# One stream of score blocks over all groups, PV per 256 queries in two accumulators, V per two groups, and an order planned with modelled engine clocks

## The chip, the cores and the metric

The kernel runs on one core of one Trainium2 chip, in one launch. The metric is the device time of the whole program in microseconds (us). The core's engines run side by side and wait for each other by semaphores: TensorE (PE, with its weight loads listed as PEld), VectorE (DVE), ScalarE (ACT), GpSimd (POOL) and SyncE (SP), which issues nearly all DMAs.

## The reference

Two problems, A and B, of the same form and independent of each other; the two results stand side by side in the output. S = 2048 tokens, D = 1024, 32 heads of 32, bf16, a causal window of 256 tokens:

```
qkv = x @ wqkv                       # [2048, 3072]; q, k, v of 32 heads of 32
scores = q @ k^T * 32**-0.5          # where 0 <= i - j < 256, else -1e9
o = softmax(scores) @ v              # per head
out = o (heads side by side) @ wo    # [2048, 1024]
```

## The kernel before

A group is four heads, 128 columns of q, k or v; a problem has T = 8 groups, the program 16 (G). The sequence is cut into 16 blocks of 128 tokens (NB) and four quarters of 512 (NQ). x is loaded transposed, a quarter a time (xT). Each projection is a chain of 8 steps over the inner dimension, and each step is four matmuls side by side, one for each 32 columns of its weights (`by_columns`, L127): q and k of a group for a quarter (`qk_steps`, L132), v for 128 tokens and four groups at once (`v_steps`, L152), and the output product (`out_steps`, L169). A chain of 512 columns sums in one PSUM bank, a tile `pp`, of which there are two; then a cast takes it to SBUF, by DVE for q and k (L145), by ACT for v and the output (L165, L183). After the cast of q or k DVE also takes the bitwise OR of it into `top` (L146), from which the kernel later decides if all q and k were small enough for a softmax without a maximum (`certify`, L571; a slow path follows if not).

The scores of a group are 45 pairs of a key block and a query block (`entries`). `session` (L276) takes four pairs, SLOTS: matmuls for the four heads into the four banks of the one tile `st`, one exponential on ACT for all of them (L298) into a tile `pt`, and masks on POOL (L303, L307). A group has 12 such score blocks, the last with a single pair: 192 in all, 16 of them with one pair. `pv` (L311) multiplies with v (and with ones, for the sums) for a quarter's 512 queries into the one tile `acc`, two banks; then DVE takes four reciprocals and two products (L342, L346) into oT, in pieces (`side`) which are handed out between projection steps.

The order is planned while the program is built. Every projection chain has an earliest and a latest score block. In front of each score block `forced` finishes what is due; behind it come the PV that is due (two blocks after its last exponential, PV_LAG), the loads, and then `emit` hands out steps up to a budget of `level` (L264): the larger of what must still be done and what may be done, spread evenly over the rest. Costs are constants per step (NS_MM, NS_QK, NS_PV). All loads and the output DMAs go through SP's queue in program order.

Of the kernel before, what the change touches and what calls it, by code (L numbers as in the profile page):

```python
# [18 lines left out]
P = 128  # L19
# [7 lines left out]
QB = 4  # L27
SLOTS = 4
NS_MM = 216.0
NS_QK = 430.0  # L30
NS_PV = 56.0
PV_LAG = 2
FREE = 10 ** 6

# [14 lines left out]
class _Chain:  # L49
    def __init__(self, early, late, steps):  # L50
        self.early, self.late, self.steps = early, late, steps


def _fast_path(ctx, tc, cfg, problems, outs, consts, certify):
# [5 lines left out]
    SB = 512 // P  # L60
    ones = consts["ones"]

    entries = [(j, q) for j in range(NB) for q in range(j, min(j + 3, NB))]
    place = {e: divmod(n, SLOTS) for n, e in enumerate(entries)}
    NS = -(-len(entries) // SLOTS)
    ready = [max(place[(j, q)][0] for (j, q) in entries if q // QB == k) for k in range(NQ)]

    def first_use(k, of):
        return min(place[e][0] for e in entries if e[of] // QB == k)
# [3 lines left out]
    wvp = ctx.enter_context(tc.tile_pool(name="wv", bufs=1))  # L73
    wopool = ctx.enter_context(tc.tile_pool(name="wo", bufs=1))
    opool = ctx.enter_context(tc.tile_pool(name="oT", bufs=NQ + 2))
# [6 lines left out]
    ps_acc = ctx.enter_context(tc.tile_pool(name="ps_acc", bufs=1, space=PSUM))  # L82
# [26 lines left out]
    def load_wv(m, queue, parts=1):  # L109
        pi, mm = divmod(m, T // SB)  # L110
        wv[m] = wvp.tile([P, CT, 512], BF16, name="wv")
        n = CT // parts
        for a in range(parts):
            queue.dma_start(out=wv[m][:, a * n:(a + 1) * n, :],
                            in_=wsrc(pi)[:, a * n:(a + 1) * n, 2, mm * 512:(mm + 1) * 512])

    def load_wo(pi):
        wo_sb[pi] = wopool.tile([P, CT, D], BF16, name="wo_sb")
        nc.sync.dma_start(out=wo_sb[pi][:],
                          in_=problems[pi][2].rearrange("(ct p) n -> p ct n", p=P))  # L120
# [6 lines left out]
    def by_columns(out, lo, hi, lhsT, rhs, start, stop):  # L127
        for c in range(0, P, 32):
            nc.tensor.matmul(out[c:c + 32, lo:hi], lhsT=lhsT[:, c:c + 32], rhs=rhs, start=start,  # L129
                             stop=stop, tile_position=(0, c))  # L130

    def qk_steps(g, which, k, lo=0, hi=512, st_=None, last=True):  # L132
        pi = g // T
        st_ = {} if st_ is None else st_
        steps = []
        for ct in range(CT):
            def f(ct=ct):
                if "pp" not in st_:
                    st_["pp"] = ps_proj.tile([P, 512], F32, name="pp")
                w_ = wqk[g][:, ct, which, :]  # L140
                by_columns(st_["pp"], lo, hi, lhsT=w_, rhs=xT[(pi, k)][:, ct, lo:hi],
                                 start=(ct == 0), stop=(ct == CT - 1))
                if ct == CT - 1 and last:
                    dst = qk_tiles(g)[which][:, k * 512:(k + 1) * 512]
                    nc.vector.tensor_copy(out=dst, in_=st_["pp"][:])  # L145
                    nc.vector.tensor_tensor(out=top[:], in0=top[:],  # L146
                                            in1=dst.bitcast(I32), op=ALU.bitwise_or)
            steps.append((NS_MM * (hi - lo) / 512.0, f))
        return steps

    def v_steps(m, b):
        pi = m // (T // SB)  # L152
# [3 lines left out]
        for ct in range(CT):  # L156
            def f(ct=ct):
                if ct == 0:
                    st_["pp"] = ps_proj.tile([P, 512], F32, name="pp")
                    if (m, k) not in vts:  # L160
                        vts[(m, k)] = vp.tile([P, QB, 512], BF16, name="vt")
                by_columns(st_["pp"], 0, 512, lhsT=xT[(pi, k)][:, ct, a * P:(a + 1) * P],
                                 rhs=wv[m][:, ct, :], start=(ct == 0), stop=(ct == CT - 1))
                if ct == CT - 1:
                    nc.scalar.copy(out=vts[(m, k)][:, a, :], in_=st_["pp"][:])  # L165
# [3 lines left out]
    def out_steps(pi, b, ch, osb):  # L169
        k, a = divmod(b, QB)  # L170
        st_ = {}
        steps = []
        for ct in range(CT):
            def f(ct=ct):
                if ct == 0:
                    st_["pp"] = ps_proj.tile([P, 512], F32, name="pp")
                    if ch == 0:
                        osb[0] = misc.tile([P, D], BF16, name="osb")
                by_columns(st_["pp"], 0, 512, lhsT=oTs[(pi, k)][:, ct, a * P:(a + 1) * P],
                                 rhs=wo_sb[pi][:, ct, ch * 512:(ch + 1) * 512],  # L180
                                 start=(ct == 0), stop=(ct == CT - 1))
                if ct == CT - 1:
                    nc.scalar.copy(out=osb[0][:, ch * 512:(ch + 1) * 512], in_=st_["pp"][:])  # L183
                    if ch == cfg.NCH - 1:
                        nc.sync.dma_start(out=outs[pi][b * P:(b + 1) * P, :], in_=osb[0][:])
            steps.append((NS_MM, f))
        return steps

    def pv_time(g, k):
        return NS * g + ready[k] + PV_LAG  # L190

    def wv_time(m):
        return pv_time(SB * (m - 1), NQ - 1) + 1 if m else 0

    def x_time(pi, k):
        if pi == 0:
            return -1
        if k < 2:
            return NS * (pi * T - 3) + 2 * k
        return NS * (pi * T - 1) + first_use(k - 2, 0) + 1  # L200

    chains = []
    for g in range(G):
        for k in range(NQ):
            for which in (0, 1):
                if g == 0 and k == 0:
                    continue
                late = NS * g + first_use(k, 1 - which) - (1 if g else 0)
                early = max(NS * (g - 1), x_time(g // T, k) + 3)
                chains.append(_Chain(early, late, qk_steps(g, which, k)))  # L210
    for m in range(NPROB * T // SB):
        for b in range(NB):
            k = b // QB
            early = max(wv_time(m) + 2, x_time(m * SB // T, k) + 3) if m else 0
            if m > 1:
                early = max(early, pv_time(SB * (m - 1) - 1, min(k + 1, NQ - 1)) + 1)
            chains.append(_Chain(early, pv_time(SB * m, k), v_steps(m, b)))
    wo_time = [0] + [NS * (pi * T + T - 3) for pi in range(1, NPROB)]
    for pi in range(NPROB):
        for b in range(NB):  # L220
            k = b // QB
            osb = [None]
            early = pv_time(pi * T + T - 1, k) + 2
            late = FREE
            if pi + 1 < NPROB:
                late = pv_time((pi + 1) * T, k + 2) if k + 2 < NQ else wo_time[pi + 1] - 1
            for ch in range(cfg.NCH):
                chains.append(_Chain(early, late, out_steps(pi, b, ch, osb)))
    chains.sort(key=lambda c: c.late)
    due = [(pv_time(g, k), g, k) for g in range(G) for k in range(NQ)]  # L230
    END = NS * G
    fixed = [NS_QK] * END
    for d, g, k in due:
        if d < END:
            fixed[d] += NS_PV * (2 * (3 * QB - (2 if k == 0 else 0)) + 2)
# [10 lines left out]
    side = []  # L246

    def emit(now, budget):
        done = 0.0
        since = 0.0  # L250
        while done < budget - 0.5 * NS_MM and (current or start_chain(now)):
# [3 lines left out]
            since += ns  # L255
            if side and since >= 3.5 * NS_MM:
                side.pop(0)()
                since = 0.0

    def forced(now):  # L260
        while any(c.late <= now for c in chains):
            emit(now, NS_MM * (len(current) or CT))
        emit(now, NS_MM * len(current) if any(c.late <= now + 1 for c in chains) else 0.0)

    def level(now):
        held = sum(ns for ns, _ in current)
        size = NS_MM * CT
        need, cap = 0.0, float("inf")
        base = 0.0
        for d in range(now + 1, END + 1):  # L270
            base += fixed[d - 1]
            must = base + held + size * sum(c.late <= d for c in chains)
            may = base + held + size * sum(c.early < d for c in chains)
            need = max(need, must / (d - now))
            cap = min(cap, may / (d - now))
        return max(need, cap)  # L276

    def session(g, s):
        qT, kT = qks[g]
        es = entries[s * SLOTS:(s + 1) * SLOTS]  # L280
        n = len(es)
        st = ps_st.tile([P, 4, 512], F32, name="st")
        a = 0
        while a < n:
            b = a
            while b < n and es[b][0] == es[a][0]:
                b += 1
            j, q0 = es[a]
            for r in range(4):
                nc.tensor.matmul(  # L290
                    st[:, r, a * P:b * P],
                    lhsT=kT[32 * r:32 * r + 32, j * P:(j + 1) * P],
                    rhs=qT[32 * r:32 * r + 32, q0 * P:(q0 + b - a) * P],
# [3 lines left out]
        pts[(g, s)] = pt  # L297
        nc.scalar.activation(out=pt[:, :, :n, :].rearrange("p r j q -> p r (j q)"),  # L298
                             in_=st[:, :, :n * P], func=ACT.Exp, bias=-SHIFT, scale=cfg.scale)
        for a, (j, q) in enumerate(es):  # L300
# [10 lines left out]
    def pv(g, k):  # L311
        pi, t = divmod(g, T)
        m, u = divmod(g, SB)
        segs = []
        for j in range(max(QB * k - 2, 0), QB * k + QB):
            for q in range(max(j, QB * k), min(j + 3, QB * k + QB)):
                s, a = place[(j, q)]
# [4 lines left out]
        acc = ps_acc.tile([P, 2, 512], F32, name="acc")  # L322
        for which in range(2):
            for x, (j, q, s, a, n) in enumerate(segs):
                o = (q - QB * k) * P
                for r in range(4):
# [3 lines left out]
                                     rhs=pts[(g, s)][:, r, a:a + n, :],  # L330
                                     start=(x == 0), stop=(x == len(segs) - 1),
# [293 lines left out]
```

## Time and profile before

| | |
|---|---|
| median of 3 runs | 688.26 us (688.08 to 689.99) |
| the profiled execution | 689.5 us, of which the span of its instructions is 687.7 us |
| PE busy | 629.0 us, 91% of the span |
| DVE busy | 426.6 us, 62% |
| ACT busy | 408.7 us, 59% |
| POOL busy | 300.5 us, 44% |
| DMA | 35.42 MB, 52 GB/s on average |
| mean granted clock of PE | 0.977 of 2.4 GHz |

A busy engine is one with a matmul, cast or the like under way. A row of the timeline gives the start and the duration of one or several instructions that follow each other, and in brackets how long the engine stood still before and who ended that. The durations that the prediction uses come from the profiled execution.

### The profile page before, as it was taken

To read this page: it belongs to the slowest core of one execution; us is meant where nothing else is said; L and a number is where in the kernel's file an instruction comes from. 1 tells how busy PE (TensorE), PEld (TensorE's weight loads), DVE (VectorE), ACT (ScalarE), POOL (GpSimd) and SP (SyncE) were. 2 spreads that over 40 slices of the span, in tenths; PEclk is the share of its full clock that TensorE was granted. 3 is DMA by queue.
4 is the path that set the end of the run, shared out by engine and by line. 5 is a ranking of instruction groups with operands and counts; after the bars stand their busy time and mean duration, and the time that the engine had idled before them with its cause. 6 is when DMAs were issued, how large, how long until landed. Compare 5 with 4: busy or idle time off the path is not lost.

```text
span 687.7 us, 28015 instructions
## 1 busy us (share of the span) xinstructions
PE 629.0 (91%) x13069; PEld 310.8 (45%) x13069; DVE 426.6 (62%) x647; ACT 408.7 (59%) x321; POOL 300.5 (44%) x484
## 2 busy tenths in 40 slices
PE   7999999999978999689999999998999987769996
PEld 4445444444434444334445444454444443434453
DVE  1364988666686849575462987748465688773220
ACT  2465556767664675546666545665776766645532
POOL 0343545545553545534443454445455566542200
PEclk9999999999998999789999999999999999989999
DMA  9920300105060107000103300000204210001121
GB/s 216 233 76 10 87 18 19 33 2 94 5 153 2 34 3 147 11 1 3 64 3 102 86 18 18 3 3 2 80 36 116 85 34 2 2 2 49 64 79 66
DMA packets 77323, 35.42 MB, mean 52 GB/s; under 512 B 66960, under 2 KB 71056, under 8 KB 77200
## 3 DMA queue, kind: packets, MB, share of 16 engines
q1 hardware_dynamic: 75120, 33.04, 19.3%
q8 instruction: 104, 1.70, 1.0%
q10 hardware_dynamic: 2080, 0.52, 0.3%
q14 instruction: 19, 0.16, 0.1%
HBM read 16.78 MB, written 8.39 MB: 37 GB/s over the span
## 4 chain that ended last, share of the span: by engine, by line
PE 64%; DVE 28%; ACT 5%; issue 1%; DMA 1%; POOL 1%; ACTq 0%
PE pp L129 45%; DVE rinv L342 14%; PE acc L329 13%; PE st L290 6%; DVE top L146 4%; ACT pt L298 4%; DVE qT L145 3%; DVE oT L346 3%; DVE kT L145 3%; DMA xT<-in_A_x_dram 1%; POOL pt L303 0%; ACT osb L183 0%; ACT vt L165 0%; POOL pt L307 0%; DVE pm L574 0%
## 5 line engine op out<-in xcount | busy, mean ns | idle before, releaser
L298 ACT ACTIVATE pt<-st 128x2048 bf16<-128x2048 f32 x192 | 340.0, 1771 | 201.1 <-PE st L290 186.9
L342 DVE RECIPROCAL rinv<-acc 128x128 f32<-128x128 f32 x256 | 231.2, 932 | 181.1 <-PE acc L329 180.8
L129 PE MATMUL pp<-xT,wqk 128*32 128x512 bf16 (+1 forms) x4160 | 253.8, 384 | 11.2 <-DVE qT L145 4.1
L307 POOL TENSOR_SCALAR_AFFINE_SELECT pt<-pt 128x512 bf16<-128x512 bf16 x224 | 146.8, 655 | 204.5 <-ACT pt L298 204.5
L303 POOL TENSOR_SCALAR_AFFINE_SELECT pt<-pt 128x512 bf16<-128x512 bf16 x256 | 167.1, 653 | 144.1 <-ACT pt L298 144.0
L129 PEld LDWEIGHTS <-wqk 128*32 128x32 bf16 x4160 | 107.8, 98 | 118.1 <-issue 36.4
L129 PE MATMUL pp<-wv,xT 128*32 128x512 bf16 x2048 | 121.9, 380 | 3.8 <-DVE qT L145 2.9
L129 PE MATMUL pp<-wo_sb,oT 128*32 128x512 bf16 x2048 | 118.1, 382 | 0.5 <-ACT osb L183 0.5
L290 PE MATMUL st<-qT,kT 32*128 32x256 bf16 (+2 forms) x1472 | 74.7, 273 | 18.1 <-ACT pt L298 16.3
L129 PEld LDWEIGHTS <-oT 128*32 128x32 bf16 x2048 | 53.0, 97 | 54.9 <-issue 6.5
L129 PEld LDWEIGHTS <-xT 128*32 128x32 bf16 x2048 | 51.7, 97 | 57.1 <-issue 11.5
L290 PEld LDWEIGHTS <-kT 32*128 32x128 bf16 x1472 | 24.7, 92 | 96.4 <-issue 94.0
L145 DVE CAST qT<-pp 128x512 bf16<-128x512 f32 x64 | 42.5, 664 | 38.4 <-PE pp L129 38.3
L329 PE MATMUL acc<-pt,vt 128*32 128x256 bf16 (+2 forms) x1664 | 53.0, 266 | 14.3 <-DVE oT L346 11.4
L183 ACT CAST osb<-pp 128x512 bf16<-128x512 f32 x64 | 37.2, 585 | 42.7 <-PE pp L129 41.1
L346 DVE TENSOR_TENSOR oT<-acc,rinv 128x256 bf16<-128x256 f32 x128 | 54.4, 425 | 4.4
L165 ACT CAST vt<-pp 128x512 bf16<-128x512 f32 x64 | 37.3, 584 | 28.2 <-PE pp L129 27.8
L329 PE MATMUL acc<-pt,ones 128*32 128x256 bf16 (+2 forms) x1664 | 53.9, 268 | 0.0
L329 PEld LDWEIGHTS <-vt 128*32 128x32 bf16 x1664 | 34.9, 98 | 32.1 <-issue 23.6
L145 DVE CAST kT<-pp 128x512 bf16<-128x512 f32 x64 | 43.0, 672 | 5.9 <-PE pp L129 5.9
L329 PEld LDWEIGHTS <-ones 128*32 128x32 bf16 x1664 | 37.6, 100 | 4.5 <-issue 0.2
L146 DVE TENSOR_TENSOR top<-top,qT 128x256 int32<-128x256 int32 x64 | 35.9, 561 | 2.2
(17 smaller groups left out, 43.9 us busy)
## 6 DMA issues: line engine op xcount, KB each, us to landing
out_dram<-osb SPq DMA_DIRECT2D x32, 256.0 KB, 2.0
wqk<-in_B_wqkv_dram SPq DMA_DIRECT2D x16, 256.0 KB, 3.7
wqk<-in_A_wqkv_dram SPq DMA_DIRECT2D x14, 256.0 KB, 3.9
wo_sb<-in_A_wo_dram SPq DMA_DIRECT2D x1, 2048.0 KB, 10.1
wv<-in_B_wqkv_dram SPq DMA_DIRECT2D x2, 1024.0 KB, 5.7
wo_sb<-in_B_wo_dram SPq DMA_DIRECT2D x1, 2048.0 KB, 10.2
wv<-in_A_wqkv_dram SPq DMA_DIRECT2D x2, 512.0 KB, 4.9
wv<-in_A_wqkv_dram SPq DMA_DIRECT2D x1, 1024.0 KB, 5.0
```

The lines of the kernel that those rows point to most:

```text
L129: nc.tensor.matmul(out[c:c + 32, lo:hi], lhsT=lhsT[:, c:c + 32], rhs=rhs, start=start, stop=stop, tile_position=(0, c))
L145: nc.vector.tensor_copy(out=dst, in_=st_["pp"][:])
L146: nc.vector.tensor_tensor(out=top[:], in0=top[:], in1=dst.bitcast(I32), op=ALU.bitwise_or)
L165: nc.scalar.copy(out=vts[(m, k)][:, a, :], in_=st_["pp"][:])
L183: nc.scalar.copy(out=osb[0][:, ch * 512:(ch + 1) * 512], in_=st_["pp"][:])
L290: nc.tensor.matmul(st[:, r, a * P:b * P], lhsT=kT[32 * r:32 * r + 32, j * P:(j + 1) * P], rhs=qT[32 * r:32 * r + 32, q0 * P:(q0 + b - a) * P],
L298: nc.scalar.activation(out=pt[:, :, :n, :].rearrange("p r j q -> p r (j q)"), in_=st[:, :, :n * P], func=ACT.Exp, bias=-SHIFT, scale=cfg.s ...
L303: nc.gpsimd.affine_select(out=blk, in_=blk, pattern=[[0, 4], [1, P]], compare_op=ALU.is_ge, fill=0.0, base=0, channel_multiplier=-1)
L307: nc.gpsimd.affine_select(out=blk, in_=blk, pattern=[[0, 4], [-1, P]], compare_op=ALU.is_gt, fill=0.0, base=0, channel_multiplier=1)
L329: nc.tensor.matmul(acc[32 * r:32 * r + 32, which, o:o + n * P], lhsT=lhsT, rhs=pts[(g, s)][:, r, a:a + n, :], start=(x == 0), stop=(x == l ...
L342: nc.vector.reciprocal(out=rinv[:, h * P:(h + 1) * P], in_=acc[:, 1, a * P:(a + 1) * P])
L346: nc.vector.tensor_tensor(out=oTs[(pi, k)][:, t, sl], in0=acc[:, 0, sl], in1=rinv[:], op=ALU.mult)
```

## The change

Score blocks now form one stream over all 16 groups: block n takes the pairs 4n to 4n + 3 of 720, so that a block may hold pairs of two groups, and there are 180, all full. PV is done for 256 queries (a pair of query blocks, NP = 8 per group) into a tile of one bank, numerators and sums side by side; there are two such tiles. V is computed for two groups at a time (VG): a chain holds two runs of 8 steps with 256 columns each, for two blocks of 128 tokens, in one bank; wv comes in tiles of half the size, of which there are two. wo is loaded in two halves, and the output leaves in pieces of 128 x 512. The certificate's DVE part and its matmul are apart. Every cast goes to ACT or DVE, whichever is done sooner by clocks that the planner keeps while it builds the program (`_Clock`); the OR and the pieces of the normalisation are handed out when DVE's clock is not ahead of PE's. The pace of projection steps is now the bound by what may be done (`cap`) alone.

The core of the diff:

```diff
+VG = 2
 NS_MM = 216.0
-NS_QK = 430.0
-NS_PV = 56.0
+NS_ROW = 420.0
+NS_PV = 52.0
+ACT_EXP = 1800.0
+COST = {"act": 590.0, "dve": 670.0, "or": 560.0, "rinv": 930.0, "mult": 430.0}
...
+class _Clock:
...
+    def chain(self):
+        self.pe = max(self.pe, self.banks.pop(0))
+
+    def evacuate(self, engines):
+        best = min(engines, key=lambda e: max(getattr(self, e), self.pe) + COST[e])
+        end = max(getattr(self, best), self.pe + 150.0) + COST[best]
+        setattr(self, best, end)
+        self.banks.append(end)
+        return best
...
-    place = {e: divmod(n, SLOTS) for n, e in enumerate(entries)}
-    NS = -(-len(entries) // SLOTS)
+    END = -(-G * NE // SLOTS)
+    def place(g, j, q):
+        return divmod(g * NE + order[(j, q)], SLOTS)
...
-    wvp = ctx.enter_context(tc.tile_pool(name="wv", bufs=1))
+    wvp = ctx.enter_context(tc.tile_pool(name="wv", bufs=2))
-    ps_acc = ctx.enter_context(tc.tile_pool(name="ps_acc", bufs=1, space=PSUM))
+    ps_acc = ctx.enter_context(tc.tile_pool(name="ps_acc", bufs=2, space=PSUM))
...
+    def evacuate(out, in_, engines=("act", "dve")):
+        if clock.evacuate(engines) == "act":
+            nc.scalar.copy(out=out, in_=in_)
+        else:
+            nc.vector.tensor_copy(out=out, in_=in_)
...
 (v_steps)
+        for h in range(512 // w_):
+            for ct in range(CT):
...
+                    by_columns(st_["pp"], h * w_, (h + 1) * w_,
+                               xT[(pi, k)][:, ct, (a + h) * P:(a + h + 1) * P],
+                               wv[m][:, ct, :], ct == 0, ct == CT - 1)
...
 (out_steps)
-                    if ch == cfg.NCH - 1:
-                        nc.sync.dma_start(out=outs[pi][b * P:(b + 1) * P, :], in_=osb[0][:])
+                    osb = misc.tile([P, 512], BF16, name="osb")
+                    evacuate(osb[:], st_["pp"][:])
+                    nc.sync.dma_start(out=outs[pi][b * P:(b + 1) * P, ch * 512:(ch + 1) * 512],
+                                      in_=osb[:])
...
 (emit)
-            since += ns
-            if side and since >= 3.5 * NS_MM:
-                side.pop(0)()
-                since = 0.0
+            if side and (clock.dve < clock.pe + 100.0 or len(side) > 8):
+                run_side()
...
 (level)
-        return max(need, cap)
+        return cap
...
 (pv)
-        acc = ps_acc.tile([P, 2, 512], F32, name="acc")
+        acc = ps_acc.tile([P, 2, 256], F32, name="acc")
+        clock.pe = max(clock.pe, clock.norms.pop(0))
...
 (the loads at the start)
-    load_wv(0, nc.sync, parts=2)
+    load_wv(0, nc.sync)
     load_x(0, 1)
     load_wqk(1, nc.sync)
     load_x(0, 2)
     load_x(0, 3)
+    load_wv(1, nc.sync)
...
-        if not certified and not current and not any(c.late < FREE for c in chains):
-            certify(top, ps_proj)
+        if now >= sealed and len(certify) == 2:
+            while side:
+                run_side()
+            certify.pop(0)(top)
+        elif now >= sealed + 2 and len(certify) == 1:
+            certify.pop(0)(ps_proj)
```

Two places show how instructions move. The first is PE behind the program's first score block (`st_276` before, `st_277` now); `xT_111` is the first quarter of x, `xT_117` and `xT_116` the second, and numbers only name buffers. Each row stands for the first of its many equal ones, and weight loads are shown once. Before:

```order
L290 MATMUL st_276<-qT_238,kT_239 128x128
L129 LDWEIGHTS xT_111
L129 MATMUL pp_290<-wv_114,xT_111 32x512
L129 MATMUL pp_325<-wv_114,xT_111 32x512
L129 MATMUL pp_359<-wv_114,xT_111 32x512
L290 MATMUL st_393<-qT_238,kT_239 128x256
```

And now:

```order
L352 MATMUL st_277<-qT_241,kT_242 128x128
L160 LDWEIGHTS wqk_108
L160 MATMUL pp_291<-xT_116,wqk_108 32x512
L160 MATMUL pp_327<-wv_114,xT_111 32x256
L352 MATMUL st_362<-qT_241,kT_242 128x256
L160 MATMUL pp_408<-xT_116,wqk_108 32x512
```

Three V chains of the first quarter stood there; now a chain of q for the second quarter comes first, and half a V chain behind it. The second place is ACT over the last groups, up to the output chains of the end; `ACTIVATE pt<-st` is a score block's exponential, and x10 means ten in a row. Before:

```order
L298 ACTIVATE pt<-st 128x2048 x10
L298 ACTIVATE pt<-st 128x4x128
L298 ACTIVATE pt<-st 128x2048 x11
L298 ACTIVATE pt<-st 128x4x128
L298 ACTIVATE pt<-st 128x2048 x7
L183 CAST osb<-pp 128x512 x3
```

And now, from the last group but one:

```order
L360 ACTIVATE pt<-st 128x2048
L173 CAST qT<-pp 128x512
L360 ACTIVATE pt<-st 128x2048 x2
L173 CAST qT<-pp 128x512
L360 ACTIVATE pt<-st 128x2048
L173 CAST kT<-pp 128x512
L360 ACTIVATE pt<-st 128x2048 x2
L173 CAST osb<-pp 128x512
```

Thirty exponentials stood there with no cast on ACT between them; now one or two stand between casts of q, k and the output, and output chains of A have moved into these groups.

## Rows read from the trace of the kernel before

**Rows 1.** The page's part 1: busy time, share and instructions of each engine.

```profile
PE 629.0 (91%) x13069; PEld 310.8 (45%) x13069; DVE 426.6 (62%) x647; ACT 408.7 (59%) x321; POOL 300.5 (44%) x484
```

**Rows 2.** Windows: length; busy PE, PEld, DVE, ACT, POOL; PE's clock, DMA, GB/s.

```profile
0.00:195.00 195.00, 186.84 (x3867) 92.07 (x3868) 124.64 (x194) 115.22 (x88) 85.28 (x140) 0.99 0.36 79
195.00:305.00 110.00, 92.58 (x1892) 46.12 (x1888) 77.05 (x118) 64.82 (x43) 54.78 (x87) 0.91 0.18 38
305.00:540.00 235.00, 225.84 (x4788) 110.26 (x4788) 145.41 (x215) 150.72 (x126) 107.69 (x172) 1.00 0.15 45
540.00:618.00 78.00, 60.33 (x1304) 30.72 (x1296) 64.02 (x100) 49.89 (x28) 44.25 (x72) 0.98 0.04 9
```

**Rows 3.** Waits, whole span: PE's longest, with total us, times, longest.

```profile
PE st L290 <- ACT pt L298: 16.3, 25, 2.1
...
PE acc L329 <- DVE oT L346: 11.4, 9, 2.2
...
PE pp L129 <- DVE qT L145: 7.1, 9, 0.9
...
PE pp L578 <- DVE okp L575: 3.7, 1, 3.7
PE pp L129 <- DVE kT L145: 3.7, 7, 0.9
```

**Rows 4.** Timeline of PE, 640 to 682: start, duration, line, instruction, count.

```profile
640.65 1.68 PE L129 MATMUL pp<-wo_sb,oT 128*32 128x512 bf16 x28
642.27 0.40 PE L290 MATMUL st<-qT,kT 32*128 32x256 bf16 x8
642.60 0.84 PE L329 MATMUL acc<-pt,vt 128*32 128x128 bf16 x28
643.26 0.83 PE L329 MATMUL acc<-pt,ones 128*32 128x128 bf16 x28
...
657.60 24.35 PE L129 MATMUL pp<-wo_sb,oT 128*32 128x512 bf16 x448
```

**Rows 5.** Timeline, 549 to 552: two score blocks in a row.

```profile
549.27 0.40 PE L290 MATMUL st<-qT,kT 32*128 32x384 bf16 x8 [0.20 <-ACT pt L298]
...
551.73 0.40 PE L290 MATMUL st<-qT,kT 32*128 32x256 bf16 x8 [0.22 <-ACT pt L298]
```

**Rows 6.** Waits of PE, 305 to 540.

```profile
PE pp L129 <- DVE qT L145: 4.2, 5, 0.9
PE pp L129 <- DVE kT L145: 3.0, 4, 0.9
```

**Rows 7.** Waits of PE, 0 to 195.

```profile
PE pp L129 <- DVE qT L145: 2.0, 3, 0.7
...
PE pp L129 <- DVE kT L145: 0.4, 2, 0.3
```

**Rows 8.** The page's part 6: output transfers, KB each, median us to landing.

```profile
out_dram<-osb SPq DMA_DIRECT2D x32, 256.0 KB, 2.0
```

**Rows 9.** Timeline, 5 to 20: SP's issues and PE at the start.

```profile
6.82 1.12 SPq L114 DMA_DIRECT2D wv<-in_A_wqkv_dram  x2
7.27 5.34 PE L129 MATMUL pp<-xT,wqk 128*32 128x256 bf16 x128 [2.07 <-DMA xT<-in_A_x_dram]
7.99 6.26 SPq L95 DMA_TRANSPOSE xT<-in_A_x_dram  x1
13.92 5.36 PE L129 MATMUL pp<-wv,xT 128*32 128x512 bf16 x96
```

**Rows 10.** DMA issues, 7.9 to 8.1: the second quarter of x, us to landing.

```profile
xT<-in_A_x_dram SPq DMA_TRANSPOSE x1, 9.7
```

**Rows 11.** Windows, columns as in Rows 2: behind PE's first wait.

```profile
7.50:10.90 3.40, 3.40 (x73) 3.17 (x65) 0.00 (x0) 0.00 (x0) 0.00 (x0) 0.50 0.94 264
```

**Rows 12.** Groups by form, whole span: busy us, mean ns | idle before.

```profile
L298 ACT ACTIVATE pt<-st 128x2048 bf16<-128x2048 f32 x176 | 330.5, 1878 | 188.9 <-PE st L290 176.3 <-POOL pt L303 7.5 <-POOL pt L307 4.8
...
L342 DVE RECIPROCAL rinv<-acc 128x128 f32<-128x128 f32 x256 | 231.2, 932 | 181.1 <-PE acc L329 180.8
...
L145 DVE CAST qT<-pp 128x512 bf16<-128x512 f32 x64 | 42.5, 664 | 38.4 <-PE pp L129 38.3
```

More of the change, by code (lines that the diff above doesn't have):

```diff
@@ L51, in __init__ @@
         self.early, self.late, self.steps = early, late, steps
+        self.size = sum(ns for ns, _ in steps)
+class _Clock:
+    def __init__(self):
+        self.pe = self.act = self.dve = 0.0
+        self.exp = 0.0
+        self.norms = [0.0, 0.0]
+        self.banks = [0.0, 0.0]
+        self.after = []
+    def chain(self):
[6 more added lines that the diff above has]
+        return best
 def _fast_path(ctx, tc, cfg, problems, outs, consts, certify):
@@ L212, in _fast_path @@
+    wo_time = {(pi, ch): 0 if pi == 0 else begin(G - 2) if ch < cfg.NCH - 1 else begin(G - 1) + 7
+               for pi in range(NPROB) for ch in range(cfg.NCH)}
+    for pi in range(NPROB):
+        final = pi == NPROB - 1
         for b in range(NB):
             k = b // QB
[L214 to L226, printed above, removed]
-            for ch in range(cfg.NCH):
-                chains.append(_Chain(early, late, out_steps(pi, b, ch, osb)))
+            for ch in range(cfg.NCH):
+                early = max(pv_time(pi * T + T - 1, 2 * k + 1) + 1, wo_time[(pi, ch)] + 2)
+                late = FREE if final else wo_time[(pi + 1, ch)] - 1
+                if not final and k < NPROB * NQ - (2 * NQ - 1):
+                    late = pv_time((pi + 1) * T, 2 * (2 * NQ - 1 - NQ + k)) - 1
+                chains.append(_Chain(early, late, out_steps(pi, b, ch)))
@@ L229, in _fast_path @@
+    assert all(c.early <= c.late for c in chains), [(c.early, c.late, c.size) for c in chains
+                                                    if c.early > c.late]
     chains.sort(key=lambda c: c.late)
[L230 to L233, printed above, removed]
+    due = [(pv_time(g, p), g, p) for g in range(G) for p in range(NP)]
+    fixed = [NS_ROW] * END
+    for d, g, p in due:
         if d < END:
-            fixed[d] += NS_PV * (2 * (3 * QB - (2 if k == 0 else 0)) + 2)
+            fixed[d] += NS_PV * (2 * (6 - (3 if p == 0 else 0)) + 2)
@@ L244, in start_chain, with run_side @@
         return False
-    side = []
+    def run_side():
+        cost, f, last = side.pop(0)
+        f()
+        clock.dve = max(clock.dve, clock.pe) + cost
+        if last:
+            clock.norms.append(clock.dve)
     def emit(now, budget):
         done = 0.0
-        since = 0.0
-        while done < budget - 0.5 * NS_MM and (current or start_chain(now)):
+        while (current or chains) and done < budget - 0.5 * (current[0][0] if current else NS_MM):
+            if not current and not start_chain(now):
+                break
             ns, f = current.pop(0)
@@ L296, in session @@
         pt = ptp.tile([P, 4, SLOTS, P], BF16, name="pt")
[L297 to L300, printed above, removed]
+        pts[now] = pt
+        nc.scalar.activation(out=pt[:, :, :n, :].rearrange("p r a q -> p r (a q)"),
+                             in_=st[:, :, :n, :].rearrange("p r a q -> p r (a q)"),
+                             func=ACT.Exp, bias=-SHIFT, scale=cfg.scale)
+        clock.act = max(clock.act, clock.pe) + ACT_EXP
+        clock.exp = clock.act
+        for a, (g, j, q) in enumerate(es):
             blk = pt[:, :, a, :]
```

249 lines of the change are left out of this document (134 added, 115 removed).

## Prediction

> **What bounds the kernel now.** I read the busy shares first, then the same by stages, then PE's waits, then single stretches of the timeline. PE is busy for 629.0 us of the 687.7 us span [rows 1]; no other engine reaches two thirds. But the stages differ: in 305 to 540 us PE is busy for 225.84 of 235, in 195 to 305 for 92.58 of 110, in 540 to 618 for 60.33 of 78, and the granted clock there is 0.91 and 0.98 instead of 1.00 [rows 2]. So the kernel has long stretches at PE's pace and two starved ones. The waits say why [rows 3]: score blocks wait for the exponential of the block before (16.3 us, with one buffer of scores), PV for the normalisation of the PV before (11.4, with one accumulator), projection chains for a cast that frees their bank (7.1 and 3.7), and the check's tiny matmul for its DVE chain (3.7). In the starved stretches a score block can't start before 2.46 us after the one before (549.27, 551.73) [rows 5]; by the program, 38 of the 192 blocks have less than 2.02 us of other matmuls behind them (2.46 less a block's own 0.44, below), some none at all.
>
> **What PE must do, before and after.** I call the four matmuls that run side by side in 32-column tiles a quad. Durations [rows 4]: 448 matmuls of 512 columns (112 quads) take 24.35 us, the last of them 0.38 to its end, so (24.35 - 0.38) / 111 = 0.216 us a quad. A full score block costs 0.33 us from its start to the next matmul (642.27 to 642.60) and 0.11 before it (642.27 less 640.65 plus 7 x 0.216), together 0.44. A PV half of 12 blocks of 128 columns takes 0.66 us in 7 quads (642.60 to 643.26), where 1536 columns at 2.4 GHz are 0.640: about 3.6 ns a quad on top of its columns.
> Before: 2032 quads of 512 x 0.216 = 438.9; 184,320 PV columns = 76.8 and 832 quads x 0.0036 = 3.0; 176 full score blocks x 0.44 = 77.4 and 16 of one block x 0.27 = 4.3, less 1.2 for six that follow another directly; first chains 5.3 [rows 9]. Sum 604.5.
> After, from the program's counts: 1520 quads of 512 = 328.3; V in 1024 quads of 256 columns; the same PV columns in 1080 quads, 76.8 + 3.9 = 80.7; 180 full blocks = 79.2; first chains 5.3. V's quads of 256 columns are not in the trace at full clock with nothing else around them: lower end 0.107 (columns alone), upper end 0.167 (128 such matmuls took 5.34 us, partly at clock 0.50 [rows 9, 11]); I take 0.110, columns and 3.6 ns, since rows 4 have wider and narrower quads at that overhead and at full clock. 1024 x 0.110 = 112.6. For PV, lower end the columns, upper end every quad at the mean of 0.66 / 7 = 0.095 us: 102.6, 22 more; I take the 80.7, as rows 4 fix the overhead of a mix of widths. Sum 606.1. So the work on PE doesn't shrink; it grows by 1.6 us.
> Fixed: first projection matmul at 7.27, 1.0 us from the end of the first chains (12.61) to the score block that ends at 13.92, less its 0.33 [rows 9], and 5.7 from the last matmul (681.95, rows 4) to the end: 14.0. Without any wait and at full clock before would take 618.5, after 620.1. Before took 687.7: **69 us are waits and their wake.** The waits of rows 3 make 42.2 of these; clock below 1.00 in three stages accounts for some 10 (110 us x 0.09 and little more); the rest I read as time that a matmul's own record covers at the start of a wait.
>
> **What the change does to each wait.** *Starved blocks.* The stream puts four blocks in each of 180 exponentials, and the pace rule spreads the chains: in the new order each block has 2.39 to 3.9 us of other matmuls behind it until the last three. With 0.44 that is a pace of 2.8 or more against 2.46, so the 16.3 us go. What hides the exponential is then that work; if a stretch lost it, each block would cost up to 2.46 less its own work, as now. *PV.* Two accumulators of 256 queries: PV waits for the one before the last, which lies two or three score blocks back, 6 to 9 us, against two reciprocals of 0.932 [rows 12] and a product; the 11.4 go. What hides the normalisation is that distance; where DVE falls a block behind, each PV would cost up to the 2.2 us that rows 3 give as the longest. *Check.* Its DVE part runs two score blocks and their long output chains ahead of its matmul, 3.7 go. *Clock.* With the gaps go the low stretches, about 10 us. *Chain banks.* Casts go to ACT or DVE by modelled clocks: 162 to ACT (128 before), 94 to DVE (128). DVE's busy time falls by 34 x 0.664 = 23 to 404 us, ACT's 408.7 rises by about as much; at some 633 us both stand near two thirds. A bank is needed one chain (1.73 us) after its end; a cast (0.664) behind one reciprocal (0.932) makes that, a cast behind an exponential (1.878) does not [rows 12]. So waits stay, and the order decides how many. What the trace gives: in 305 to 540, 7.2 us of waits for DVE casts, 3.1% [rows 6]; in 0 to 195, 2.4 us of 181 after the start, 1.3% [rows 7]. Over 580 us these are 18 and 7.5; below, nothing, if the choice always finds a free engine. I take 7.5: the early stretch has the even pace that the whole program gets.
> *Start: a new wait.* Behind the first score block stood three V chains, which read the x block that is already there; now a Q chain of the second x block stands there. That transfer is issued at 7.99 and lands 9.7 us later, 17.7 [rows 9, 10]; it is issued half of wv's 1.12 us earlier and has half a megabyte less ahead of it, so I take 17.0. PE is ready at 13.92: a wait of 3.1, and behind it in PE's queue stand all V chains and the second score block. After the 2.07 us wait before 7.27 the clock was at 0.50, the 1.2 GHz level, for 3.4 us [rows 9, 11]; the same again costs 1.7. Together 4.8; ends: nothing if the smaller load lets it land at once, 5.5 if at 17.7.
> *Output.* 64 transfers of half the size, two buffers: each buffer comes back after two chains, 3.46 us, against 2.0 to land [rows 8]; hidden. Without that cover each of some 20 last chains would lose up to 0.6. SP's other issues keep their places between PE's chains; none moves ahead of a load that waits longer.
>
> **Sum.** 620.1 + 4.8 + 7.5 = 632.4 span. The profiled execution of before took 689.5 at a span of 687.7, 1.8 outside; 634.2 in the same terms. The median of the runs is 688.26, 0.2% below the profiled one: 633.
>
> **Rivals.** (a) The cast waits stay at the worse rate of today and ACT's and DVE's fuller queues add PV and score waits: 18 instead of 7.5 and some 5 on top, 649. For: both engines at two thirds, in strict order. Against: rows 7. (b) Each PV quad costs the mean 0.095: +22, 655. For: quads of 128 rise from 352 to 720. Against: the 0.66 us, in which quads of 128 stand too.
> Beside (b) stands a rule of the Trainium skill, "TensorE: Matmul & The Clock Gate" (Part 1, "Wait — 56ns, not 53.3ns?"): start to start never falls below about 25 ns, however few the columns. By that floor a quad of 128 columns would cost 100 ns instead of 57, and 720 of them against 352 would add an estimated 16 us, 649 in all. The trace speaks against it for tiles side by side: 28 matmuls in 0.66 us, wide ones among them, are 23.6 ns each [rows 4].
> (c) Slower: V's quads are bound by their four weight loads instead of by their columns and cost as much as 512-wide ones, 0.216: 1024 x 0.106 = 108 more, 741; the sign turns at 0.164 a quad, and at the startup's 0.167 it is 691. For: V's matmuls double to 4096, each with a weight load of its own. Against: the PV quads of rows 4, with as many loads to a column and more, run at their columns' rate. (d) The planner's clocks are off and one starved stretch stays, as in 195 to 305: 17 us in which PE is not busy and up to 10 of clock [rows 2], 660.
>
> **Chances.** Forecast 0.70, (a) 0.17, (b) 0.05, (c) 0.03, (d) 0.05. The forecast's own range is 622 (no cast wait, no wait at the start) to 643 (cast waits of 18). To leave out no more than 2 in 10 on either side I go to 653, which takes in (a): 622 to 653. 0.3%, 2.1 us, is about what a measurement of this kernel can tell from no change. Faster by more: forecast, (a), (b), (d) and a little of (c), 0.96; within it 0.01; slower 0.03.
>
> **What would show it.** PE's busy time near 620 and a span about 13 above; clock 1.00 in every stage after the start; score waits for ACT below 3 us, PV waits for DVE below 3; a PE wait for the x transfer of 2 to 4 us at 14 us with clock 0.50 behind it; V matmuls of 256 columns at 110 ns a quad. It is wrong if cast waits pass 20 us, if a new wait (PV for POOL, output buffers) passes 10, or if a V quad takes over 0.13.

## The result, and the profile after

The changed kernel took 629.25 us, the median of four runs (627.98 to 634.16), against 688.88 before (four runs beside it): a ratio of 0.915, 95% interval 0.909 to 0.920. The forecast was 633, with a range of 622 to 653. Two later repeats, each beside eleven runs of before, gave 631.06 and 631.72 (ratios 0.918 and 0.916). Two of the six runs of experiment 7 fell in a slower state and are left out of its median and ratio. The profiled execution is the slowest of the first four, 634.16 us with a span of 632.4; what that means for the working is told below.

Part 1 of the page of the changed kernel, as in [rows 1]:

```profile
PE 613.3 (97%) x16125; PEld 368.9 (58%) x16125; DVE 405.4 (64%) x613; ACT 427.6 (68%) x343; POOL 306.6 (48%) x484
```

PE has 15.7 us less busy time, though its work is a little more, and the span 55.3 less: the rest was idleness. Its waits over the whole span, to be laid beside [rows 3]; these are all of them:

```profile
PE pp L160 <- DMA xT<-in_A_x_dram: 5.0, 2, 3.0
PE pp L160 <- issue: 4.2, 4, 1.6
PE acc L396 <- issue: 2.1, 1, 2.1
PE pp L450 <- DVE top L120: 1.3, 1, 1.3
PE st L352 <- ACT kT L173: 0.7, 1, 0.7
```

Nothing is left of the waits for an exponential, a normalisation, a cast that frees a bank or the check's DVE part (the last two rows are of the start: a first matmul behind the clearing of `top`, and the first score block behind the cast of its k). The wait for x is new in part (2.0 of the 5.0 stood there before, [rows 9]), and two rows of "issue" are quite new: there PE waited for nothing that the profile shows. The windows, columns as in [rows 2], four stages and two short stretches:

```profile
30.00:195.00 165.00, 159.62 (x4404) 98.07 (x4404) 112.18 (x171) 117.64 (x91) 87.75 (x139) 0.99 0.23 52
195.00:305.00 110.00, 109.19 (x3076) 67.44 (x3072) 81.93 (x124) 83.85 (x66) 61.88 (x96) 1.00 0.22 48
305.00:500.00 195.00, 194.81 (x5220) 115.66 (x5212) 140.82 (x213) 140.51 (x108) 105.30 (x165) 1.00 0.16 41
500.00:565.00 65.00, 65.00 (x1684) 37.00 (x1676) 44.23 (x65) 46.24 (x37) 34.41 (x55) 1.00 0.08 28
...
178.20:181.60 3.40, 3.40 (x40) 1.14 (x36) 2.80 (x6) 0.63 (x2) 0.44 (x1) 0.50 0.02 5
17.80:21.20 3.40, 3.40 (x56) 1.71 (x48) 1.12 (x2) 0.00 (x0) 0.00 (x0) 0.50 1.30 271
```

The stretch of 195 to 305, where PE was busy for 92.58 us at clock 0.91, is now full at 1.00. While PE works, three short stretches lie at the 1.2 GHz level, each behind a wait: one at 7.6 us, as before [rows 11], and the two shown last. PE's timeline shows the start (as [rows 9]), the V chains, and the place of the largest new stalls:

```profile
13.26 0.40 PE L352 MATMUL st<-qT,kT 32*128 32x384 bf16 x8 [0.69 <-ACT kT L173]
16.64 2.53 PE L160 MATMUL pp<-xT,wqk 128*32 128x512 bf16 x32 [2.99 <-DMA xT<-in_A_x_dram]
...
24.69 1.92 PE L160 MATMUL pp<-wv,xT 128*32 128x256 bf16 x64
26.44 0.60 PE L160 MATMUL pp<-xT,wqk 128*32 128x512 bf16 x8
...
167.78 1.70 PE L160 MATMUL pp<-wv,xT 128*32 128x256 bf16 x56
171.09 0.40 PE L160 MATMUL pp<-wv,xT 128*32 128x256 bf16 x8 [1.60 <-issue]
...
174.60 0.35 PE L396 MATMUL acc<-pt,vt 128*32 128x128 bf16 x8
177.01 0.35 PE L396 MATMUL acc<-pt,vt 128*32 128x256 bf16 x8 [2.06 <-issue]
```

The 64 V matmuls, 16 quads, take 26.44 - 24.69 = 1.75 us, 0.109 a quad. The large stalls called "issue" stand in and right behind V chains. Part 3 of both pages has the transfers that bring instructions to the engines (queue, kind, packets, MB, share). Before:

```profile
q8 instruction: 104, 1.70, 1.0%
```

And the changed kernel:

```profile
q8 instruction: 128, 2.10, 1.3%
```

Each is 16 KB; there are 24 more, since V's and PV's narrower quads need 3056 more matmuls and as many weight loads: 6112 instructions, 255 a transfer.

### The profile page after: what moved, and what is told of

Its sections match the earlier page's. It is cut to its first block, busy times and chain, and to the rows that moved or that the text cites. A ratio compares the mean times of both kernels' runs of the same rounds, so it can differ in the third digit from the quotient of the medians.

```text
span 632.4 us, 34301 instructions
## 1 busy us (share of the span) xinstructions
PE 613.3 (97%) x16125; PEld 368.9 (58%) x16125; DVE 405.4 (64%) x613; ACT 427.6 (68%) x343; POOL 306.6 (48%) x484
## 4 chain that ended last, share of the span: by engine, by line
PE 95%; DMA 1%; issue 1%; SPq 1%; ACT 1%; POOL 0%; ACTq 0%
PE pp L160 71%; PE acc L396 15%; PE st L352 9%; DMA xT<-in_A_x_dram 1%; SPq L127 1%; ACT pt L360 0%; ACT vt L173 0%; POOL pt L372 0%; POOL pt L368 0%; ACT osb L173 0%; SPq L145 0%; ACTq L173 0%
## 5 line engine op out<-in xcount | busy, mean ns | idle before, releaser
L372 POOL TENSOR_SCALAR_AFFINE_SELECT pt<-pt 128x512 bf16<-128x512 bf16 x224 | 149.4, 667 | 180.9 <-ACT pt L360 180.9
L368 POOL TENSOR_SCALAR_AFFINE_SELECT pt<-pt 128x512 bf16<-128x512 bf16 x256 | 170.5, 670 | 106.3 <-ACT pt L360 106.3
L160 PE MATMUL pp<-wv,xT 128*32 128x256 bf16 x4096 | 129.4, 274 | 3.2 <-issue 3.2
L160 PEld LDWEIGHTS <-xT 128*32 128x32 bf16 x4096 | 107.2, 97 | 17.8 <-issue 7.7
L352 PE MATMUL st<-qT,kT 32*128 32x384 bf16 (+2 forms) x1488 | 71.9, 270 | 0.7 <-ACT kT L173 0.7
L396 PE MATMUL acc<-pt,vt 128*32 128x128 bf16 (+1 forms) x2160 | 63.7, 239 | 2.1 <-issue 2.1
L396 PE MATMUL acc<-pt,ones 128*32 128x128 bf16 (+1 forms) x2160 | 62.1, 237 | 0.0
L173 ACT CAST osb<-pp 128x512 bf16<-128x512 f32 x49 | 28.7, 586 | 37.8 <-PE pp L160 34.3
L167 DVE TENSOR_TENSOR top<-top,qT 128x256 int32<-128x256 int32 x64 | 34.6, 541 | 14.4 <-ACT qT L173 12.5
L167 DVE TENSOR_TENSOR top<-top,kT 128x256 int32<-128x256 int32 x64 | 35.9, 561 | 7.1 <-ACT kT L173 5.2
L173 ACT CAST qT<-pp 128x512 bf16<-128x512 f32 x40 | 23.4, 585 | 24.3 <-PE pp L160 23.7
L173 ACT CAST kT<-pp 128x512 bf16<-128x512 f32 x43 | 25.2, 585 | 13.0 <-PE pp L160 12.3
```

Source lines behind the costliest of these rows:

```text
L167: nc.vector.tensor_tensor(out=top[:], in0=top[:], in1=dst.bitcast(I32), op=ALU.bitwise_or)
L173: nc.scalar.copy(out=out, in_=in_)
L352: nc.tensor.matmul(st[:, r, a:b, :], lhsT=kT[32 * r:32 * r + 32, j * P:(j + 1) * P], rhs=qT[32 * r:32 * r + 32, q * P:(q + b - a) * P], st ...
L368: nc.gpsimd.affine_select(out=blk, in_=blk, pattern=[[0, 4], [1, P]], compare_op=ALU.is_ge, fill=0.0, base=0, channel_multiplier=-1)
L372: nc.gpsimd.affine_select(out=blk, in_=blk, pattern=[[0, 4], [-1, P]], compare_op=ALU.is_gt, fill=0.0, base=0, channel_multiplier=1)
L396: nc.tensor.matmul(acc[32 * r:32 * r + 32, which, o:o + n * P], lhsT=lhsT, rhs=pts[s][:, r, a:a + n, :], start=(which == 0 and x == 0), st ...
```

## The experiments

"The changed kernel" is the base of all but the third and the fourth. They came in three groups (1 to 4, 5 to 8, 9 to 11), each with runs of the kernel before. The changed kernel itself ran in the last two (runs 6 and 11); runs 1 and 2 are set against it by the ratios to before, which for the changed kernel are 0.915 to 0.918.

**1. Casts bound to engines.** q and k to DVE, V and the output to ACT, as before:

```diff
-                    evacuate(dst, st_["pp"][:])
+                    evacuate(dst, st_["pp"][:], ("dve",))
...
-                    evacuate(osb[:], st_["pp"][:])
+                    evacuate(osb[:], st_["pp"][:], ("act",))
```

> The changed kernel, with the casts bound to engines as before: q and k on DVE, V and output on ACT. Order of PE unchanged. Theory (the choice of engine is what removes the waits for chain banks): cast waits of PE return at the rate of 305 to 540 us before, 3.1 to 3.8%, 18 to 22 us; about 647 to 651 us in all. Rival (the even pace alone removes them): under 5 us of cast waits, at most 635.

It took 640.39 us (ratio to before 0.930, 0.928 to 0.932): by the ratios 8 to 11 more than the changed kernel, between the two expectations. Its waits:

```profile
PE pp L160 <- issue: 3.2, 6, 1.8
PE acc L396 <- issue: 2.9, 1, 2.9
PE pp L160 <- ACT vt L173: 2.8, 6, 0.6
PE pp L160 <- ACT osb L173: 1.9, 4, 0.5
...
PE pp L160 <- DVE kT L175: 0.7, 1, 0.7
```

Cast waits are back, mostly on the engine with the exponentials, but they make 5.4 us, not 18 to 22. Against run 6's profile the span is 8.9 us longer (638.1 to 629.2): the 5.4, 2.0 more of issue stalls and 2.6 more of PE's busy time, less 0.7 of waits for x, make 9.3, near enough. So the free choice is worth some 1.5% here.

**2. One accumulator.**

```diff
-    ps_acc = ctx.enter_context(tc.tile_pool(name="ps_acc", bufs=2, space=PSUM))
+    ps_acc = ctx.enter_context(tc.tile_pool(name="ps_acc", bufs=1, space=PSUM))
...
-            finish_norm(1)
+            finish_norm()
```

> The changed kernel with one PV accumulator of 256 queries instead of two (the normalisation of one PV is issued in full before the next PV). Theory (the second accumulator is what removes PV's waits): PV directly in the next block finds the normalisation (about 2.3 us of DVE, and what DVE has in front of it) not done; 60 to 70 such places at 0.1 to 0.3 us, 8 to 20 us, 637 to 650 in all, PV waits for DVE of that size. Rival (PV per 256 queries at an even pace doesn't need it): under 3 us, at most 633.

(The planner's clock has one accumulator too.) It took 656.76 us (ratio 0.953, 0.950 to 0.955), by the ratios 24 to 26 more. The wait that it brings:

```profile
PE acc L396 <- DVE oT L413: 21.0, 35, 1.2
```

The direction is as expected, the size above it: with PV per 256 queries there are 128 normalisations to wait for instead of 64, and at PE's full pace DVE is late for 35 of them, by 0.6 us on average, where 60 to 70 of 0.1 to 0.3 were expected. The finer PV needs the second accumulator; the 11.4 us of [rows 3] don't tell its worth.

**3 and 4. The kernel before with the new pace alone, and with wo of problem B two groups later as well.** The later load keeps A's output chains for the last groups.

```diff
-        return max(need, cap)
+        return cap
...
 (the fourth only)
-    wo_time = [0] + [NS * (pi * T + T - 3) for pi in range(1, NPROB)]
+    wo_time = [0] + [NS * (pi * T + T - 1) for pi in range(1, NPROB)]
```

> The kernel before, with one line of the change: the pace is the bound by what may be done, no longer the larger of that and what must be done. By the program starved score blocks fall from 38 to 29, all in the last groups. Theory (starved blocks and the low clock behind them make half of the gain): score waits in 195 to 305 us go, clock there near 1.00, some 20 us less than before, 665 to 672. Rival (bank and accumulator waits make the gain, starved blocks were only where they showed): no less than 682.

> The same, and wo of problem B is loaded two groups later (at the start of the last group), so that output chains of A may stand in the last groups; 7 starved blocks by the program. Theory: the second starved stage goes too, another 12 to 17 us, 650 to 657; what is left to the changed kernel's 629 is PV's waits for its accumulator, bank waits and the check. Rival: as before, no less than 675.

They took 672.19 us (ratio 0.977, 0.973 to 0.980) and 659.58 (0.959, 0.956 to 0.962). The waits of the third:

```profile
PE acc L329 <- DVE oT L346: 8.6, 7, 1.9
PE pp L129 <- DVE kT L145: 6.8, 15, 0.7
PE st L290 <- ACT pt L298: 4.6, 18, 0.5
```

And of the fourth:

```profile
PE pp L129 <- DVE kT L145: 7.9, 17, 0.7
PE pp L129 <- DVE qT L145: 4.4, 8, 1.5
PE pp L578 <- DVE okp L575: 3.8, 1, 3.8
PE pp L129 <- ACT vt L165: 3.4, 8, 0.5
```

Both are slower than their forecasts, the third by a hair (665 to 672), the fourth by 2.6 us (650 to 657), and far from the rivals (682, 675). Two edits of the planner, with no new tile or chain, give 17 and 13 of the 60 us: score waits fall from 16.3 to 4.6 us, then below 1. What stays is what the change's other parts take away: waits for casts (16.4 us in the fourth with 0.7 for the output's, not shown) and for the check.

**5. V first.** The wait at 14 us stood where the forecast put it, so the next question was whether another order removes it. No q or k chain of a later quarter of x comes before block 1:

```diff
-                early = max(-(-(g - 1) * NE // SLOTS), x_time(g // T, k) + 3)
+                early = max(-(-(g - 1) * NE // SLOTS), x_time(g // T, k) + 3, 1)
```

> The changed kernel with the q and k chains of all later x quarters not before the second score block, so that V chains of the first quarter fill the stretch behind the first one. Theory (the 3.0 us wait for the second quarter of x and the 1.7 us of low clock behind it are real cost): no such wait at 14 to 17 us, clock 1.00 there, 3 to 5 us less than the changed kernel in the same call, some 624 to 626. Rival (the work is only put elsewhere: later q and k chains come nearer to their due time and score blocks or casts wait instead): within 1.5 us of the changed kernel.

It took 630.45 us; the changed kernel beside it (run 6) 631.06. PE's timeline:

```profile
11.76 2.26 PE L160 MATMUL pp<-wv,xT 128*32 128x256 bf16 x76
15.53 1.60 PE L160 MATMUL pp<-wv,xT 128*32 128x256 bf16 x52 [1.52 <-issue]
...
25.08 2.75 PE L160 MATMUL pp<-xT,wqk 128*32 128x512 bf16 x24 [3.27 <-DMA xT<-in_A_x_dram]
```

The rival's time holds, 0.6 us apart, but neither score blocks nor casts wait: the wait moved from the second quarter of x to the third, and an issue stall of 1.5 us appeared in the V chains that now stand there.

**6. The changed kernel again** (no edit).

> The changed kernel once more, beside the kernels it is compared with. Theory (PE's stalls that the trace puts down to issue come from its instruction stream arriving late while the DMA engines are full): they come again, 4 to 7 us in all, at 35 and near 170 us, with the clock at 0.50 behind the later ones; time 627 to 632. Rival (a chance event of the one profiled execution): stalls of that kind under 2 us or at other places; time then 625 to 628.

631.06 us. Issue stalls of 4.1 us at 35, 169, 173 and 373 us, so they belong to the program and not to one execution. One part of the theory failed: the clock behind the later ones stayed at 1.00 (in run 11 it fell to 0.50 for 3.4 us).

**7. q and k chains in two runs of 256 columns.** The same columns, 25% more matmuls:

```diff
-                chains.append(_Chain(early, late, qk_steps(g, which, k)))
+                st_ = {}
+                chains.append(_Chain(early, late, qk_steps(g, which, k, 0, 256, st_, False)
+                                     + qk_steps(g, which, k, 256, 512, st_, True)))
```

> The changed kernel with q and k chains (all but the first quarter of group 0) in two runs of 8 steps of 256 columns, as V has them: 4032 more matmuls and as many weight loads, the same columns. By 3.6 ns a quad PE's work grows by 1008 x 0.0036 = 3.6 us. Theory (the stream of instructions limits PE where DMA is full): the issue stalls grow with the number of instructions, from about 6 to 9 us or more, time 8 us or more above the changed kernel. Rival (instructions are cheap, the stalls have another cause): 3 to 5 us above it, issue stalls as before. Third (narrow quads carry more than 3.6 ns): PE's busy time grows by over 8 us without stalls.

It took 664.0 us, the median of four runs (658.33 to 666.86; ratio 0.962, 0.959 to 0.966), 33 more than run 6. The issue stalls of the profiled one, of 666.86 us:

```profile
PE pp L160 <- issue: 16.2, 24, 3.0
...
PE acc L398 <- issue: 3.6, 6, 1.1
PE st L354 <- issue: 2.0, 3, 1.2
```

And its instruction transfers, from part 3 of its page:

```profile
q8 instruction: 159, 2.61, 1.6%
```

The stalls make 21.8 us, and PE's busy time 17 above run 6 (627.9 against 611.2; the forecast's 3.6 ns a quad would give 3.6): the first theory, by far more than it expected. The third's sign, busy time up by over 8 us, shows as well, but most of that is stops too: a matmul's record, 0.28 us long on average, covers the start of one. Read from start to start, the stops where a block of instructions ends (run 9 shows where that is) grow by about 26 us against run 6, 8 more than the issue rows show, and the low clock takes 2 more. 31 more transfers for 8064 more instructions are 260 each.

**8. Plain transfers for B's x.**

```diff
+            if pi:
+                nc.sync.dma_start(out=t_[:].rearrange("p c n -> p (c n)"),
+                              in_=problems[pi][0][k * 512:(k + 1) * 512, :].rearrange(
+                                  "(p a) d -> p (a d)", p=P))
```

B's x then stands untransposed, and B's output is not the reference's.

> The changed kernel with x of problem B loaded by plain contiguous transfers instead of transposing ones (B's x is then not transposed; the sizes and the order of all work are the same). Theory (the issue stalls at 160 to 180 us come from instruction fetches that stand behind the transposing transfers): no issue stall and no low clock between 160 and 185 us, 4 to 6 us less than the changed kernel; the one at 35 us, beside problem A's transposes, stays. Rival (the fetches are late for another reason): the stalls near 170 us stay, time within 1.5 us of the changed kernel.

628.37 us (628.19 to 628.51), 2.7 less than run 6, between theory and rival. All of its issue stalls:

```profile
PE pp L166 <- issue: 2.5, 3, 1.5
```

The stall of 2.1 us at 173 to 175 is gone, the one near 169 stays at 0.5 (0.5 in run 6 too), the one at 35 stays. So the largest stall does hang on the transposing transfers, of which two are issued from 162 us on in the changed kernel; the rest of the stalls don't. By the packets' start times it is the transfer of instructions that begins late: 3.5 us after PE went on from the stall before in the changed kernel's profile, 3.7 in run 6, 1.1 here. Whether the transposing does it or only its length is open: with plain transfers the DMA share from 170 to 180 us is 0.03, in run 6 it is 0.47.

**9. V in quads of 128 columns** (V's sums are not the reference's here, two runs alternate in one bank):

```diff
-                    by_columns(st_["pp"], h * w_, (h + 1) * w_,
+                    for u in range(0, w_, P):
+                        by_columns(st_["pp"], h * w_ + u, h * w_ + u + P,
```

> The changed kernel with every V quad of 256 columns issued as two of 128: 4096 more matmuls and weight loads, the same columns and the same order otherwise. Theory from the run with split q and k chains (instructions reach PE at no more than one transfer of 16 KB, some 256 of them, every 3.4 to 3.5 us, 13.5 ns each; a quad is eight): two quads of 128 take up to 16 x 13.5 = 216 ns where the instructions ahead are used up, and 114 where some are in store; 1024 x 0.10 = up to 105 us more, less what the wide chains and score blocks between refill: 660 to 720, with issue stalls inside or behind the V chains. Rival (columns plus 3.6 ns a quad; the stalls of the split kernel came from its other order): 3.7 us more, 632 to 638. Third (every matmul at least 25 ns): 1024 x 2 x 0.043 = 88 more, near 718, evenly, without a stall: V matmuls exactly 25 ns apart from the first one of a chain on.

713.82 us, 82 more than the changed kernel beside it and slower than before (ratio 1.035, 1.031 to 1.038). Its issue stalls:

```profile
PE pp L160 <- issue: 54.0, 46, 3.1
PE acc L397 <- issue: 6.9, 9, 1.6
...
PE st L353 <- issue: 5.3, 4, 1.8
```

Two stretches of PE's timeline:

```profile
68.16 1.97 PE L160 MATMUL pp<-wv,xT 128*32 128x128 bf16 x128
69.96 1.04 PE L160 MATMUL pp<-xT,wqk 128*32 128x512 bf16 x16
...
465.82 1.64 PE L160 MATMUL pp<-wv,xT 128*32 128x128 bf16 x104 [1.23 <-issue]
467.39 0.40 PE L353 MATMUL st<-qT,kT 32*128 32x128 bf16 x8
467.71 0.51 PE L397 MATMUL acc<-pt,vt 128*32 128x128 bf16 x16
469.84 0.51 PE L397 MATMUL acc<-pt,ones 128*32 128x128 bf16 x16 [1.61 <-issue]
470.18 1.74 PE L160 MATMUL pp<-wv,xT 128*32 128x128 bf16 x112
473.31 0.74 PE L160 MATMUL pp<-wv,xT 128*32 128x128 bf16 x40 [1.39 <-issue]
```

At 68.16 wide chains stand before the V chain, and 128 matmuls take 1.80 us: 56 ns a quad, 14 a matmul, the 57 of columns and 3.6 ns. At 470, in a run of V chains, the same quads stop for 1.4 us. That is neither the second nor the third theory, and the time lies in the first one's range.

The stops stand at fixed places. From 465.82 to the stop before 469.84 there are 104 + 8 + 16 = 128 matmuls, from there to the next 16 + 112 = 128 again; with their weight loads that is 256 instructions, one block of 16 KB (160 transfers here and 128 in the changed kernel, for 8192 more instructions, are 256 each). All 59 issue stalls of this run lie whole multiples of 128 matmuls apart, and so do the 33 of run 7 and those of each of the changed kernel's three profiles (171.09 to 177.01 above, for one, is 128). PE stops where a block ends. The window of 458 to 479, columns as in [rows 2]:

```profile
458.00:479.00 21.00, 14.24 (x824) 11.84 (x810) 9.70 (x16) 9.17 (x7) 8.32 (x14) 1.00 0.02 5
```

And what was transferred in it, all of it:

```profile
q8 instruction: 6, 0.10, 2.0%
```

Nothing else is transferred there, and still PE gets 1634 matmuls and weight loads in 21 us, 12.9 ns each, from six blocks of 16 KB, one every 3.5 us. By the packets' start times each transfer begins some 1.1 us after PE has gone on, and PE goes on again 2.3 to 2.9 us after that. The supply of instructions is the bound, with empty DMA queues too. (PE's busy time is 20 us above run 11's, for 3.7 foreseen; as in run 7, that holds stops and low clock.) That the store holds some hundreds is read from the 1.80 us; how many exactly stays open.

**10. No chain of a later quarter of x early.** Run 5's idea for all quarters and for V as well:

```diff
+                ... , (0, 1, 3, 4)[k])     # in early of q, k and of V chains
```

> The changed kernel with no q, k or V chain of the second, third or fourth quarter of A's x ahead of score block 1, 3 or 4 of the program. The run with V first only moved the wait from the second quarter of x (3.0 us) to the third (3.3). Theory (at the start PE waits for x only because chains of a quarter still on its way stand too early): the wait for the first half quarter stays (2 us), the other falls under 1 us, 3 to 4 us less than the changed kernel, 625 to 628. Rival (the loads set the start, and what is not waited for there is waited for later): within 1.5 us of the changed kernel.

629.20 us (626.47 to 632.18; ratio to before 0.914, 0.911 to 0.917), beside 631.72 of the changed kernel (run 11). The profiled one took 627.01:

```profile
PE pp L160 <- issue: 5.1, 4, 1.9
PE pp L160 <- DMA xT<-in_A_x_dram: 1.6, 2, 1.0
PE acc L396 <- issue: 1.5, 1, 1.5
```

The wait for x is down to 1.6 us and the clock is 1.00 in the first 30. But an issue stall of 1.9 us came in before 16.06 us, in the V chains that now stand there; the median gains 2.5 us, not 3 to 4, and the intervals of the two overlap: the kernel is not shown to be faster than the changed one. Half of its runs lie at 626.5 to 627.7, half at 630.7 to 632.2.

**11. The changed kernel a third time.**

> The changed kernel a third time, beside the two others of this call: 629 to 632, issue stalls of 4 to 7 us near 35 and 170 us.

631.72 us (629.86 to 632.44); issue stalls of 3.6 us in its profile, at 36, 173 and 252, a little less than expected.

## Why the prediction came out as it did

*PE's work.* Of the profiled span of 632.4 the new waits take 3.0 (x) and 6.3 (issue), the two stretches at clock 0.50 half of their 3.4 us each, 3.4 together. That leaves 619.7, where the working had a floor of 620.1. V's quads took 0.109 us against 0.110, the PE work was right, and rivals (b) and (c) fell. One sign was missed: PE's busy time is 613.3 and not near 620, the span 19.1 above it and not 13; 9.3 of the 19.1 are the wait for x and the stalls. Of the waits of before, the working overlooked 4.9 us in the view of [rows 3], for masks on POOL (2.9) and for casts on ACT (1.5 and 0.5), and put them down to what records cover; they went with the rest. The Trainium skill's floor of about 25 ns from start to start ("TensorE: Matmul & The Clock Gate", Part 1, "Wait — 56ns, not 53.3ns?"), by which the working came to an estimated 649, doesn't hold for four tiles side by side: 14 ns in run 9.

*Waits that go.* Right as put: score, PV and check waits are 0 in the trace, and the clock is at 1.00 from 195 to 565 us. Runs 3 and 4 show the pace and the late wo as causes of 30 of the 60 us, run 2 shows what the second accumulator holds back, run 1 that the choice of engine for casts is worth 8 to 11. The last 20 or so were not separated by a run. The fourth run's waits say what lay in them: 16.4 us for casts, of which 5.4 come back when the choice is taken away (run 1), so 11 went with the new order; 3.8 for the check, 2.2 for a normalisation; and PE's busy time fell by 10 more, against which stand the new wait for x and the stalls.

*The start.* Predicted 3.1 us of wait and 1.7 of clock; measured 3.0 and 1.7 (the rows at 16.64 and 17.80 above). That the wait was 3.0 is in part luck: in runs 6 and 11 the first chains went at full clock (3.68 us instead of 5.34), and PE waited 4.4 and 4.5 us. What holds is the time at which x is there: PE went on at 16.64 here, at 16.25 and 16.66 there, the working had 17.0. The wait can't simply be moved away (run 5), though it can be shortened (run 10).

*Chain banks.* This term failed: "I take 7.5", measured 0. The rate of [rows 7] came from a kernel whose casts are bound to engines; with the choice one was free in time every time, the lower end that the working named. With casts bound it is 5.4 in the new order (run 1).

*What the working did not have.* Issue stalls, 6.3 us in the profiled run, with 1.7 of clock behind them: 8.0 where 7.5 was put down for casts. So the sum met the profiled run to the tenth for half a wrong reason. The stalls differ from run to run (4.1 us in run 6, with no low clock behind and a span of 629.2), and the median of 629.25 lies 4.9 below the profiled run; as far as the profiles tell, that, not an error of the floor, is why the forecast was 3.75 too high. The narrow quad was weighed as columns, weight loads and a floor per matmul, never as eight instructions that have to arrive: 8 x 12.9 = 103 ns at run 9's supply, against the 109 that a V quad takes. The change thus sits right at that edge. With V split once more the kernel is slower than before, rival (c)'s sign, by another mechanism: 713.82 us in run 9.

*Cover.* Output transfers land in 1.7 us (2.0 before, [rows 8]). Two casts of the output wait for one (3.9 us on DVE, 1.7 on ACT), but PE waits for none of it, as put.

## What to carry to other kernels

Find the starved stretches by windows before counting work: half of the gain came from spreading chains that were there, with two edits of the planner. A narrower matmul costs its columns and little more only while its instructions arrive; count instructions per microsecond of PE time as a resource of its own, and where that is near the supply, wide chains between narrow ones would be the thing to try (not tried here). A wait that disappears in one place needs the trace of the next late thing: here the x quarter, then the instruction stream.

## What the runs showed of the hardware

Instructions come in blocks of 16 KB, 256 matmuls and weight loads each, and where PE used them up, one every 3.5 us (six in 21 us in run 9); PE stops where a block ends, every 128 matmuls or a multiple of it (runs 7 and 9). From 56.5 to 90.8 us of run 7 nine came, one every 3.8, for 2380 matmuls and weight loads at 14.4 ns each. The Trainium skill ("Runtime: NRT & Kernel Launch", "Instruction fetch mechanics") gives the same block, 16 KiB and 256 instructions, and calls the cost of crossing one mostly hidden. The size agrees (256 by run 9, 260 by run 7); that it is hidden doesn't, where quads are narrow: 66 us of stalls in run 9, 22 in run 7, 3.6 to 6.3 in the changed kernel. With transposing transfers under way one stall of 2.1 us came on top, and went with them (run 8).
